# Turning five weights by DMA during the forward chain and loading them plainly later

## The chip, the core and the metric

The kernel runs on one core of one Trainium2 chip. The core has TensorE (PE), VectorE (DVE), ScalarE (ACT), GpSimd (POOL) and SyncE (SP). SP does no arithmetic here; its in-order queue issues DMAs. POOL does copies and issues DMAs as well, from one in-order queue for both. The metric is the device time of one execution in microseconds (us); lower is better. The kernel before took 2935.06 us, the median of three runs from 2926.3 to 2940.95.

## The reference

The reference is a layer of a transformer with a recurrent memory, and its gradients. The forward part, cut to what matters:

```python
h  = x  + A(layernorm(x))          # attention with memory, 64 segments of 32 tokens
h2 = h  + (silu(hn @ w_gate) * (hn @ w_up)) @ w_down     # hn = layernorm(h)
# A, for each segment s:
hs = concat([mem, xs])             # 8 memory tokens + 32 tokens, 448 features
q, k, v = hs @ Wq, hs @ Wk, hs @ Wv                      # 16 heads of 256
o = softmax(mask(q k^T / 16)) v @ Wo
mem = o[:8]                        # goes into segment s + 1
outs.append(o[8:])
```

The kernel returns h2 and the gradients of x, mem0, Wq, Wk, Wv, Wo, w_gate, w_up and w_down for a given `grad_out`. There are 2048 tokens, so 64 segments; Wq, Wk and Wv are 448 x 4096, Wo is 4096 x 448, w_gate and w_up are 448 x 1792, w_down is 1792 x 448; all are bfloat16.

The gradients need weights turned: the gradient of the gate's and the up product's input is `dgp @ w_gate^T + du @ w_up^T`, and that of a segment's input is `dv @ Wv^T + dk @ Wk^T + dq @ Wq^T`. These five turned weights are what the change is about.

## The kernel before

The kernel has four parts, one after another: the forward chain of 64 attention steps, the feed-forward part over 16 tiles of 128 tokens (its forward and its gradients together), the backward chain of 64 steps, and a tail that computes the gradients of the weights. The order of the instructions is written out by hand (`tc.manual_schedule()`); the framework only adds the waits that the data ask for. The parts are Python generators, so that one part's loads and first units stand inside the end of the part ahead of it (`next(feed)`, `next(back)`).

On chip there are four large regions for weights, W[0] to W[3] (`wall` in the profile), and an arena (`arena`) whose layout is a text of names and sizes per part: FWD, FFN, BWD and TAIL. The same bytes serve another purpose in each part, so a later part's write waits for the last reader of an earlier one. In FWD, V_sb lies at 54016 to 58112; in FFN those bytes belong to du and dgp.

**A forward step** (line 785 on, s from 0 to 63; t is the tile of 128 tokens, r the step within it) runs so:

- At its head POOL copies the memory tokens' k and q into kT and qT (L807, L808), and the four memory rows of v are moved by DMA into V_sb (`v_b_rows`, L751), from SP, in step 0 from POOL.
- PE projects k and q (L558), turns them (L572), projects v (L566) and computes the scores (L603). v comes out as 4 x 32 partitions and must stand as 2 x 32 partitions in V_sb, so it is shifted in pieces (`v_shift`): half 0 by POOL (L524) and by DMA from SP (`D_`, L755), half 1 by DMA, ACT and DVE.
- SP stores Kev and Qev to KtokA and QtokA (L858, L859).
- The softmax runs on DVE and ACT (L851 to L867); P is turned on PE (L876) and stored from POOL (L891); SP stores V_sb to Vtok (L894, two DMAs), which the backward chain reads.
- PE multiplies P with V_sb (L910) and the result with Wo (L687), and the sums of the memory tokens go into the next step's input (L616).
- Between these stand units of the next tile's memory-token projections, which fill PE's waits.
- After every fourth step POOL stores OTA and OTB (L959, L960).

**The first border.** `ff.load_turned` (L1010, L1011) stands in step 61 and loads w_down turned; it issues four transposing DMAs from SP. In step 62 the first tile of the feed-forward part is loaded. In step 63 POOL issues the plain loads of w_gate and w_up (`load_first`, L1000, L1002) and SP those of `load_rest`: w_down plainly (L1019), w_gate and w_up turned into W[2] (L1020, L1021). Behind them on SP stands the last step's Vtok store.

**The feed-forward part** takes some 19 us a tile: gate and up (L1105), the down product (L1157), the gradients dgp and du (`grads`, L1168 to L1174), their turning (L1143) and the gradient of the input (`dh_mm`, L1185), then the layer norm's gradient (L215 to L228) and its stores (DH, L1192). From the fourth tile on SP turns OTA blocks by DMA (L1220), and POOL stores them (L1221).

**The second border.** Wo (L1030), Wv, Wk and Wq (`load_back`, L1034) are loaded turned, from the inputs in DRAM, by transposing DMAs on SP's queue, in halves, each as soon as the region under it is free: Wv over gate's and up's weights, Wk over the FFW buffers and w_down, Wq over the turned gate and up. The backward step's `w_pass` (L1392) reads all three. In the backward chain, SP turns V by DMA as well (L1511, two DMAs a step).

The code that the change touches:

Of the kernel before, what the change touches and what calls it, by code (L numbers as in the profile page):

```python
# [10 lines left out]
BF16 = mybir.dt.bfloat16  # L11
# [4 lines left out]
P = 128  # L16
# [84 lines left out]
xtmp:1024x2 x2load:1024x2 P_sb1:1024 S_sb:640x2 maskr:640 maskf:160 hB#1:256"""  # L101
# [164 lines left out]
def run_all(k: _K):  # L266
    nc, tc, ctx = k.nc, k.tc, k.ctx
# [5 lines left out]
    Wq2 = aps["A_Wq"].rearrange("d h e -> d (h e)")  # L273
# [22 lines left out]
    def ps3(n=3):  # L296
# [51 lines left out]
              OTA=OTA, OTB=OTB, OTok=OTok, DHb=DHb, dxnT=dxnTd, memT=memTd, dmemT=dmemTd, memtok=memtok, dmemtok=dmemtok, dQA=dQA, dKA=dKA, dVA=dVA, dQB=dQB, dKB=dKB, dVB=dVB, doutT=doutTd, P_all=P_all)  # L348
    k.dr = dr
# [45 lines left out]
    with tc.manual_schedule():  # L395
# [86 lines left out]
        feed = ffn_phase(k, WT, ff, ffn, mv2, rstd2, {"o": Wo2, "v": Wv2, "k": Wk2, "q": Wq2}, back)  # L482
        k.feed = feed
        forward_chain(k, hA, NWIN, Wq_sb, Wk_sb, Wv_sb, Wo_sb, maskr, fwd, fwd, ff, feed)
# [9 lines left out]
def forward_chain(k: _K, hA, NWIN, Wq_sb, Wk_sb, Wv_sb, Wo_sb, maskr, work, stage, ff, feed):  # L494
# [259 lines left out]
    def D_(out, in_):  # L754
        nc.sync.dma_start(out=out, in_=in_)  # L755

# [28 lines left out]
    for s in range(NSEG):  # L785
# [22 lines left out]
        nc.gpsimd.tensor_copy(out=qT[:, :, SEG:L], in_=T.qB[:, :, r * M:(r + 1) * M])  # L808
        final = s == NSEG - 1
        if not final:  # L810
            v_b_rows(s, V_sb)
# [28 lines left out]
        v_shift(V_sb, Vev, 0, (2, 3), A if final else D_)  # L840
# [16 lines left out]
        v_shift(V_sb, Vev, 1, (0,), G_ if final else D_)  # L857
# [35 lines left out]
        for gg in range(2):  # L893
            nc.sync.dma_start(out=dr["Vtok"][s, gg], in_=V_sb[QB * gg:QB * gg + 48, :])  # L894
# [68 lines left out]

    uo["e3"]()
# [12 lines left out]
class _FFN:  # L977
# [35 lines left out]
    def load_rest(self):  # L1013
# [6 lines left out]
        nc.sync.dma_start_transpose(out=self.WgT, in_=k.aps["B_w_gate"])  # L1020
        nc.sync.dma_start_transpose(out=self.WuT, in_=k.aps["B_w_up"])  # L1021


def load_back(k, v, src, head, c0=0, c1=None):
# [8 lines left out]
    else:  # L1033
        nc.sync.dma_start_transpose(out=v[:, c0:c1, :], in_=src[:, c0 * P:c1 * P])  # L1034


def ffn_phase(k: _K, WT, ff, work, mv2, rstd2, srcs, back):
# [218 lines left out]
    for i in range(NT - 2):  # L1256
# [26 lines left out]
        if i == NT - 3:  # L1283
# [3 lines left out]
            load_back(k, WT["v"], srcs["v"], False, 0, HC)  # L1287
            up(n2)
            load_back(k, WT["v"], srcs["v"], False, HC, 2 * HC)
# [20 lines left out]
    load_back(k, WT["k"], srcs["k"], False, 0, HC)  # L1310
# [3 lines left out]
    load_back(k, WT["k"], srcs["k"], False, HC, 2 * HC)  # L1314
# [8 lines left out]
    load_back(k, WT["q"], srcs["q"], False, 0, 14)  # L1323
    dh_mm(q, (1,))
    load_back(k, WT["q"], srcs["q"], False, 14, 2 * HC)
# [756 lines left out]
```

## Time and profile before

| what | value |
|---|---|
| median of three runs | 2935.06 us |
| profiled execution | 2936.97 us, span 2935.2 us |
| PE busy | 2722.7 us, 93% of the span |
| DVE, ACT, POOL busy | 53%, 37%, 26% of the span |
| granted TensorE clock, mean | 0.980 |
| DMA | 515.86 MB in 652001 packets |
| forward step, steady | about 13.9 us |
| backward step, steady | about 14.5 us |

A profile is one execution. PE counts as busy while a matmul is in flight. A row of the instructions in order of time gives the start and the length in us, the engine and the line, the operation, the tiles written and read, and in brackets the engine's idle time ahead of it with what ended it; SPq stands for SP's queue, and its times are those of issuing, not of the transfer. A row of waits gives the total in us, how many there were, and the longest. A row of stretches gives the busy time and the count of instructions of each engine, then the granted clock, the mean busy share of the 16 DMA engines, and GB/s. The kernel's steps follow one another by data (each memory comes out of the step ahead), so a late piece in a step shows as idle time of PE in that step.

### The profile page before, as it was taken

Reading aid. Unit: us, or ns where it says so; the run is one execution under the profiler, and the core shown is the slowest. Engines: PE = TensorE matmul, PEld = TensorE weight load, DVE = VectorE, ACT = ScalarE, POOL = GpSimd, SP = SyncE. Lnnn points to the kernel's source line nnn. Section 1 sums busy time; section 2 is a strip of 40 time slices with the busy share of each in tenths; the row PEclk is TensorE's granted clock in tenths of the full one; section 3 lists DMA queues with packets and bytes.
Section 4 is the critical chain, followed back from the end, with each engine's and each line's share of the span. In section 5 each row is a group of like instructions: output and inputs, shape, how many; then the busy total and the mean of one; then the engine's idle time right before and its main releaser. Section 6 shows DMA issues by size and latency. Waiting matters only on the chain.

```text
span 2935.2 us, 104407 instructions
## 1 busy us (share of the span) xinstructions
PE 2722.7 (93%) x44384; PEld 1514.8 (52%) x44420; DVE 1561.3 (53%) x4196; ACT 1082.5 (37%) x2880; POOL 762.1 (26%) x1420
## 2 busy tenths in 40 slices
PE   3999999999998799987999999999999999999999
PEld 1555555555554455543555555555555454545454
DVE  4666666666665578874666666666665112222221
ACT  2444444444443455552444444434433111111110
POOL 2222222222222223321222222222222222233222
PEclk7999999999999899998999999999999999999999
DMA  9334434343435899997655655565556999999992
GB/s 273 116 123 134 126 123 137 116 130 122 135 116 140 217 218 233 245 226 166 151 156 153 189 152 161 155 175 152 161 151 215 334 228 227 209 225 241 204 224 69
DMA packets 652001, 515.86 MB, mean 176 GB/s; under 512 B 508592, under 2 KB 558112, under 8 KB 642000
## 3 DMA queue, kind: packets, MB, share of 16 engines
q1 hardware_dynamic: 600640, 309.09, 47.5%
q0 software_dynamic: 50896, 200.09, 20.5%
q8 instruction: 350, 5.73, 0.8%
q14 instruction: 115, 0.94, 0.1%
HBM read 145.89 MB, written 230.33 MB: 128 GB/s over the span
## 4 chain that ended last, share of the span: by engine, by line
PE 69%; DVE 15%; DMA 7%; issue 5%; SPq 2%; ACT 2%; POOL 1%; DVEq 0%; ACTq 0%; POOLq 0%
PE psf L1919 13%; PE psf L558 9%; PE psf L1392 9%; DVE arena L1355 5%; PE psf L687 4%; PE psf L1880 4%; PE psf L1105 3%; PE psf L1701 3%; PE psf L566 3%; PE psf L1364 2%; PE psh L572 2%; PE psf L1932 2%; PE psf L910 2%; PE psf L1399 2%; DMA wall<-in_A_Wv_dram 2%
## 5 line engine op out<-in xcount | busy, mean ns | idle before, releaser
L1919 PE MATMUL psf<-wall,arena 128*128 128x512 bf16 (+1 forms) x1788 | 390.6, 373 | 1.9
L521 ACT CAST arena<-psf 128x512 bf16<-128x512 f32 (+2 forms) x560 | 235.8, 453 | 362.4 <-PE psf L558 251.3
L1392 PE MATMUL psf<-wall,arena 128*32 128x448 bf16 x6144 | 336.8, 361 | 17.0 <-DMA wall<-in_A_Wq_dram 11.9
L1358 ACT CAST arena<-psf 128x256 bf16<-128x256 f32 (+1 forms) x597 | 233.0, 417 | 304.2 <-PE psf L1364 214.0
L558 PE MATMUL psf<-wall,arena 112*32 112x512 bf16 x5120 | 308.9, 384 | 31.0 <-DMA wall<-in_A_Wk_dram 14.0
L1919 PEld LDWEIGHTS <-arena 128*128 128x128 bf16 x1824 | 176.2, 98 | 198.3 <-issue 4.7
L1807 DVE CAST arena<-psf 128x448 bf16<-128x448 f32 (+1 forms) x83 | 54.7, 659 | 418.7 <-PE psf L1919 267.1
L518 DVE CAST arena<-psf 128x512 bf16<-128x512 f32 (+2 forms) x432 | 191.8, 469 | 123.7 <-PE psf L558 83.8
L1392 PEld LDWEIGHTS <-arena 128*32 128x32 bf16 x6144 | 154.9, 98 | 135.7 <-issue 30.7
L558 PEld LDWEIGHTS <-arena 112*32 112x32 bf16 x5120 | 126.4, 97 | 161.8 <-issue 28.2
L1355 DVE CAST arena<-psf 128x256 bf16<-128x256 f32 (+1 forms) x339 | 164.8, 486 | 83.0 <-PE psf L1701 41.8
L1805 ACT CAST arena<-psf 128x512 bf16<-128x512 f32 (+1 forms) x75 | 42.2, 563 | 427.9 <-PE psf L1919 267.0
L566 PE MATMUL psf<-wall,arena 112*32 112x512 bf16 x2560 | 169.2, 385 | 9.4 <-DMA wall<-in_A_Wv_dram 9.4
L1364 PE MATMUL psf<-wall,arena 128*32 128x512 bf16 x2560 | 156.6, 381 | 1.2 <-DVE arena L1404 1.2
L521 ACT COPY arena<-psh 40x160 bf16<-40x160 bf16 (+2 forms) x320 | 119.2, 400 | 94.6 <-PE psh L670 52.8
L1752 POOL COPY arena<-arena 128x32 bf16<-128x32 bf16 x63 | 13.2, 210 | 541.5 <-DVE arena L1404 541.5
L1701 PE MATMUL psf<-arena 40*128 40x40 bf16 x6144 | 146.9, 178 | 3.2 <-issue 1.8
L687 PE MATMUL psf<-wall,arena 128*32 128x224 bf16 x5120 | 147.6, 265 | 1.1 <-issue 1.1
L524 POOL COPY arena<-arena 32x512 bf16<-32x512 bf16 x129 | 77.8, 603 | 267.9 <-ACT arena L521 264.2
L1701 PEld LDWEIGHTS <-arena 40*128 40x128 bf16 x6144 | 125.8, 93 | 33.8 <-issue 16.2
L1355 DVE COPY arena<-arena 32x512 bf16<-32x512 bf16 x384 | 133.8, 349 | 8.8
L1355 DVE COPY arena<-psf 128x192 f32<-128x192 f32 x64 | 22.9, 358 | 215.2 <-ACT arena L1358 215.2
(223 smaller groups left out, 4475.5 us busy)
## 6 DMA issues: line engine op xcount, KB each, us to landing
Vtok<-arena SPq DMA_DIRECT2D x128, 192.0 KB
KtokA<-arena SPq DMA_DIRECT2D x64, 256.0 KB
QtokA<-arena SPq DMA_DIRECT2D x64, 256.0 KB
OTA<-arena POOLq DMA_DIRECT2D x16, 1024.0 KB, 5.2
arena<-QtokA SPq DMA_DIRECT2D x128, 128.0 KB
arena<-KtokA SPq DMA_DIRECT2D x128, 128.0 KB
dVA<-arena POOLq DMA_DIRECT2D x16, 1024.0 KB, 5.2
dKA<-arena POOLq DMA_DIRECT2D x16, 1024.0 KB, 7.2
```

The costliest lines, as they stand in the source:

```text
L518: nc.vector.tensor_copy(out=out, in_=in_)
L521: nc.scalar.copy(out=out, in_=in_)
L558: nc.tensor.matmul(ps[32 * g:32 * g + 32, :], lhsT=stat(kc), rhs=W_sb[0:DB, kc, c0:c0 + HB], start=(kc == 0), stop=(kc == KC - 1))
L566: nc.tensor.matmul(ps[32 * g:32 * g + 32, :].rearrange("t (y d) -> t y d", y=2), lhsT=stat(kc), rhs=wv[:, x, :, half, e, :], start=(kc == ...
L687: nc.tensor.matmul(ps[32 * g:32 * g + 32, 0:2 * DB], lhsT=x, rhs=Wo_sb[:, c, a * 2 * DB:(a + 1) * 2 * DB], start=first, stop=last)
L1355: nc.vector.tensor_copy(out=out, in_=in_)
L1358: nc.scalar.copy(out=out, in_=in_)
L1364: nc.tensor.matmul(ps[32 * g:32 * g + 32, :], lhsT=stat(kc), rhs=WoT_sb[:, kc, c0:c0 + HB], start=(kc == 0), stop=(kc == KC - 1))
L1392: nc.tensor.matmul(pO[32 * g:32 * g + 32, 0:D], lhsT=ch(c), rhs=WT[:, c, :], start=(first and i < 4), stop=(last and i >= MC - 4), skip_gr ...
L1701: nc.tensor.matmul(po[:, n * L:(n + 1) * L], lhsT=lhs[b:b + L, lc:lc + P], rhs=rhs[b:b + L, hh, 0:L], start=True, stop=True)
L1880: nc.tensor.matmul(ps[:, 0:D], lhsT=stat[:, i, c * P:(c + 1) * P], rhs=Y[:, i, 0:D], start=(i == 0), stop=(i == kts - 1))
L1919: nc.tensor.matmul(ps[:, 0:N], lhsT=Hx[:, i, dc * P:(dc + 1) * P], rhs=X[:, i, b * N:(b + 1) * N], start=(i == 0), stop=(i == kts - 1))
```

## The change

In 62 of the first 63 forward steps (all but step 61), behind the step's Vtok store, SP now issues one transposing DMA (`w_turn`): 256 columns of w_gate, w_up, Wv, Wk or Wq (448 x 256, 224 KB) land turned in a new buffer `wturn`, of which there is one. At the head of the next step, behind the two copies L807 and L808, POOL stores that buffer to a new DRAM tensor (`w_store`). There are 7 + 7 + 16 + 16 + 16 = 62 pieces.

At the borders the turned loads of these five weights (`load_rest`, `load_back`) become plain loads from those DRAM tensors, at the same places in the queue of SP. The turned loads of w_down and Wo stay.

In the last two steps, moves leave SP's queue: the v rows of the memory tokens for steps 62 and 63 go out from POOL; in step 62 two pieces of v's half 0 are copied by ACT and one piece of half 1 by POOL, as step 63 did already; and step 63's two Vtok stores go out from POOL, behind P_all.

```diff
+@76032 wturn:1792"""
+    WTd = {w: dram.tile([n, D], BF16, name="WTd_" + w) for w, n in (("g", F), ("u", F), ("v", HD), ("k", HD), ("q", HD))}
+    dr["WT"] = {w: x.rearrange("(c p) d -> p c d", p=P) for w, x in WTd.items()}
...
-            eng = nc.gpsimd if s == 0 else nc.sync
+            eng = nc.gpsimd if s == 0 or s >= NSEG - 2 else nc.sync
             eng.dma_start(out=V_sb[QB * gg + SEG:QB * gg + L, g2 * GF:(g2 + 1) * GF],
...
+    ahead = [(w, c) for w, n in (("g", k.FC), ("u", k.FC), ("v", MC), ("k", MC), ("q", MC)) for c in range(0, n, 2)]
+    held = []
+
+    def w_store():
+        for w, c, b in held:
+            nc.gpsimd.dma_start(out=dr["WT"][w][:, c:c + 2, :], in_=b)
+        held.clear()
+
+    def w_turn():
+        w, c = ahead.pop(0)
+        b = work.tile([P, 2, D], BF16, name="wturn", bufs=1)
+        nc.sync.dma_start_transpose(out=b, in_=wsrc[w][:, c * P:(c + 2) * P])
+        held.append((w, c, b))
...
         nc.gpsimd.tensor_copy(out=qT[:, :, SEG:L], in_=T.qB[:, :, r * M:(r + 1) * M])
+        w_store()
         final = s == NSEG - 1
+        ending = s >= NSEG - 2
...
-        v_shift(V_sb, Vev, 0, (2, 3), A if final else D_)
+        v_shift(V_sb, Vev, 0, (2, 3), A if ending else D_)
...
-        v_shift(V_sb, Vev, 1, (0,), G_ if final else D_)
+        v_shift(V_sb, Vev, 1, (0,), G_ if ending else D_)
...
         for gg in range(2):
-            nc.sync.dma_start(out=dr["Vtok"][s, gg], in_=V_sb[QB * gg:QB * gg + 48, :])
+            (nc.gpsimd if final else nc.sync).dma_start(out=dr["Vtok"][s, gg], in_=V_sb[QB * gg:QB * gg + 48, :])
+        if s != NSEG - 3 and ahead:
+            w_turn()
...
-        nc.sync.dma_start_transpose(out=self.WgT, in_=k.aps["B_w_gate"])
-        nc.sync.dma_start_transpose(out=self.WuT, in_=k.aps["B_w_up"])
+        nc.sync.dma_start(out=self.WgT, in_=k.dr["WT"]["g"])
+        nc.sync.dma_start(out=self.WuT, in_=k.dr["WT"]["u"])
...
-        nc.sync.dma_start_transpose(out=v[:, c0:c1, :], in_=src[:, c0 * P:c1 * P])
+        nc.sync.dma_start(out=v[:, c0:c1, :], in_=src[:, c0:c1, :])
...
-            load_back(k, WT["v"], srcs["v"], False, 0, HC)
+            load_back(k, WT["v"], dr["WT"]["v"], False, 0, HC)
...
```

The other five calls of `load_back` for v, k and q change in the same way.

More of the change, by code (lines that the diff above doesn't have):

```diff
@@ L491, in run_all, with forward_chain @@
     wts.close()
-def forward_chain(k: _K, hA, NWIN, Wq_sb, Wk_sb, Wv_sb, Wo_sb, maskr, work, stage, ff, feed):
+def forward_chain(k: _K, hA, NWIN, Wq_sb, Wk_sb, Wv_sb, Wo_sb, maskr, work, stage, ff, feed, srcs):
     nc, tc = k.nc, k.tc
@@ L962, in forward_chain @@
         late = cur
+    assert not ahead and not held
     uo["e3"]()
```

17 lines of the change are left out of this document (9 added, 8 removed).

## The prediction

> **What bounds the kernel now.** I read the busy time by stretches first, then the waits of TensorE (PE), then the instructions in order of time where PE stood still.
>
> ```profile
> 0.00:50.00 50.00, 11.61 (x92) 4.89 (x93) 22.26 (x70) 7.95 (x17) 9.31 (x23) 0.83 0.98 282
> 120.00:880.00 760.00, 733.67 (x15269) 424.82 (x15261) 496.67 (x1565) 366.88 (x924) 183.35 (x393) 1.00 0.41 126
> 1060.00:1240.00 180.00, 177.03 (x1207) 92.80 (x1206) 146.41 (x245) 99.14 (x178) 59.45 (x112) 0.99 0.95 240
> 1300.00:1350.00 50.00, 29.45 (x448) 15.04 (x446) 19.69 (x49) 12.64 (x34) 6.47 (x13) 0.69 1.09 193
> ```
>
> The columns are the stretch and its length, the busy time of PE, PE's weight loads, DVE, ACT and POOL, the granted clock, the DMA share and GB/s. In the steady forward stretch (120 to 880 us) PE is busy 733.67 of 760 us with the DMA engines at 0.41; in the feed-forward stretch 177.03 of 180. Both are PE-bound, so only their borders can give time back. The second border, 1300 to 1350, has PE busy 29.45 of 50 us at a clock of 0.69 with the DMA engines full. PE's standstills have three places.
>
> First border, the queues of POOL and SyncE (SP), DVE's wait and PE in order of time:
>
> ```profile
> 953.40 0.79 POOL L1000 DMA_DIRECT2D wall<-in_B_w_gate_dram  x1 [0.99 <-PE psf L558]
> ...
> 961.37 22.80 SPq L1020 DMA_TRANSPOSE wall<-in_B_w_gate_dram  x1
> 984.26 12.54 SPq L1021 DMA_TRANSPOSE wall<-in_B_w_up_dram  x1
> 996.90 0.98 SPq L894 DMA_DIRECT2D Vtok<-arena  x2
> ...
> DVE arena L1170 <- DMA Vtok<-arena: 13.7, 1, 13.7
> ...
> 1003.37 3.41 PE L1105 MATMUL psf<-wall 64*128 64x448 bf16 x8 [13.12 <-DVE arena L1118]
> 1006.58 3.11 PE L1143 MATMUL psh<-ident,arena 128*128 128x128 bf16 x28
> ...
> 1021.79 5.88 PE L1105 MATMUL psf<-wall 128*128 128x448 bf16 x32
> 1027.51 1.73 PE L1143 MATMUL psh<-ident,arena 128*128 128x128 bf16 x28
> ```
>
> The turned loads of gate and up hold SP from 961.37 to 996.80. Behind them stands the last step's Vtok store. Its source lies where the feed-forward part writes dgp (L1170), so DVE waits 13.7 us, stops evicting, and PE stands 13.12 us.
>
> The last two forward steps, SP and PE:
>
> ```profile
> 926.85 7.79 SPq L1010 DMA_TRANSPOSE arena<-in_B_w_down_dram  x3
> 936.71 3.76 SPq L751 DMA_DIRECT2D arena<-arena  x4
> ...
> 909.56 0.54 PE L910 MATMUL psf<-arena 104*128 104x80 bf16 x8 [1.01 <-DMA arena<-arena]
> 911.17 3.02 PE L687 MATMUL psf<-wall,arena 128*32 128x224 bf16 x64
> 926.28 1.72 PE L687 MATMUL psf<-wall,arena 128*32 128x224 bf16 x64
> 944.74 0.43 PE L910 MATMUL psf<-arena 104*128 104x80 bf16 x4 [6.00 <-DMA arena<-arena]
> 946.71 3.18 PE L687 MATMUL psf<-wall,arena 128*32 128x224 bf16 x64
> 963.34 3.51 PE L687 MATMUL psf<-wall,arena 128*32 128x224 bf16 x101
> ```
>
> In step 62 the moves into V_sb (L751, then L755) stand on SP behind the turned w_down (L1010), and L910 waits 6.00 us for them. From one L687 block to the next is 15.11 us for step 61, 20.43 for step 62, 16.63 for step 63.
>
> The border to the backward chain, SP, DVE and PE:
>
> ```profile
> 1264.20 28.18 SPq L1034 DMA_TRANSPOSE wall<-in_A_Wv_dram  x2
> 1310.66 11.43 SPq L1034 DMA_TRANSPOSE wall<-in_A_Wk_dram  x1
> 1322.20 15.61 SPq L1034 DMA_TRANSPOSE wall<-in_A_Wq_dram  x2
> ...
> 1309.08 0.69 DVE L228 SCALAR_TENSOR_TENSOR arena<-arena,rstd 128x448 f32<-128x448 f32 x1 [4.19 <-DMA DH<-arena]
> ...
> 1299.36 2.81 PE L1185 MATMUL s_ps<-wall 128*128 128x448 bf16 x14
> 1310.85 1.03 PE L1370 MATMUL psh<-ident,arena 128*128 128x128 bf16 x8 [3.90 <-DVE arena L1355]
> 1332.08 0.94 PE L1392 MATMUL psf<-wall,arena 128*32 128x448 bf16 x8 [4.97 <-DMA wall<-in_A_Wq_dram]
> 1339.97 2.43 PE L1392 MATMUL psf<-wall,arena 128*32 128x448 bf16 x24 [6.96 <-DMA wall<-in_A_Wq_dram]
> 1370.83 3.21 PE L1392 MATMUL psf<-wall,arena 128*32 128x448 bf16 x64
> ```
>
> But for a few loads between, SP is occupied with the turned Wv, Wk and Wq from 1264.20 until 1337.81. PE waits for Wq 4.97 + 6.96 us, and before that 3.90 us for DVE, itself 4.19 us late for a store of DH in the full DMA engines.
>
> **The change part by part.** The sum is made against the profiled execution: 2936.97 us, span 2935.2, so 1.8 us lie around the span. The median shown, 2935.06, is 1.91 lower.
>
> *First border.* Gate and up become two plain loads, and the last Vtok store goes to POOL's queue behind P_all. The standstill of 13.12 us goes. The half clock behind it goes too: eight matmuls of L1105 took 3.41 us where 32 take 5.88 (8: 1.47), and 28 transposes 3.11 where they take 1.73; that is 1.94 + 1.38 = 3.3. Together 16.4 us. What is late next: the plain gate and up, first used by the gradient matmuls behind those 28 transposes, that is at 1006.58 + 3.11 − 16.4 = 993.3. With Wd, Wg and Wu some 8 MB have to come from 953.40 on; at the 282 GB/s of the first 50 us, also a stretch of weight loads, that is 28 us, until 982. It fits by 11 us. Lower bound: nothing of the 3.3, and a few us of wait for these loads; 10.
>
> *End of the forward chain.* For steps 62 and 63 the V moves leave SP: the four row moves (L751) go to POOL's queue, two pieces to ACT, one to POOL. The 6.00 us wait goes. Step 61, less its half-clock loss of 3.02 − 1.72 = 1.30, is 13.8 us; two more ACT copies stand ahead of the exponentials of step 62, and I put 1.2 us for them (POOL's pair of such copies takes 1.26, in the rows of L524 below). So step 62 becomes 15.0 instead of 20.43: 5.4 us. Step 63 may also lose its half clock (101 matmuls in 3.51 us; at 1.72 for 64 it would be 2.7): I take 0.6. Together 6.0, bounds 2 (DMA engines still full of w_down, so that POOL's moves land late) and 7.
>
> *Second border.* Six turned loads become six plain ones, each issued in well under 1 us, so each starts when its target is free. PE's waits of 4.97 and 6.96 go, and DVE's 4.19, which carries the 3.90. The remaining 56 of the L1392 matmuls ran at half clock: 24 in 2.43 us where 64 take 3.21, that is 1.2 us too many in 24 and 2.8 in 56. The first backward step is thin, so I count half, 1.4. Together 4.97 + 6.96 + 4.19 + 1.4 = 17.5, bounds 12 and 20. What is late next: Wq, 3.67 MB, the targets of whose halves become free where the last but one and the last 14 matmuls of L1185 end (1299.4 and 1302.2). At 282 GB/s it needs 13 us and lands at about 1315. Its first use stands at 1332.08 − 4.97 = 1327.1 now, 1323 with DVE's 4.19 gone, perhaps 1320 at full clock: covered by 5 us.
>
> *The price in the forward chain.* 62 of the 63 other steps turn a piece of 224 KB on SP and store it from POOL. One instruction and, one step on, one store each:
>
> ```profile
> 503.44 0.86 SPq L894 DMA_DIRECT2D Vtok<-arena  x2
> 517.79 0.85 SPq L894 DMA_DIRECT2D Vtok<-arena  x2
> 521.54 2.71 SPq L751 DMA_DIRECT2D arena<-arena  x4
> ...
> 509.58 0.40 POOL L808 COPY arena<-arena 128x256 bf16<-128x256 bf16 x1
> 513.41 1.26 POOL L524 COPY arena<-arena 32x512 bf16<-32x512 bf16 x2 [3.44 <-ACT arena L521]
> 521.82 0.40 POOL L808 COPY arena<-arena 128x256 bf16<-128x256 bf16 x1
> 527.70 1.26 POOL L524 COPY arena<-arena 32x512 bf16<-32x512 bf16 x2 [5.48 <-ACT arena L521]
> ...
> 1093.83 5.61 SPq L1220 DMA_TRANSPOSE wall<-OTA  x3
> 1099.88 0.54 POOL L1221 DMA_DIRECT2D OTok<-wall  x1 [7.55 <-DMA wall<-OTA]
> ...
> PE psf L910 <- DMA arena<-arena: 6.2, 11, 1.6
> ```
>
> SP: up's 14 columns took 12.54 us, so a piece of two is 1.8. It goes out behind Vtok, at 518.64, and SP is free at 520.4, before L751 at 521.54: nothing. POOL: the store stands behind L808, from 522.2 on, and waits until the piece has landed; behind it stand POOL's V copies (L524). A turned OTA block of 256 KB, issued at 1093.83 with the DMA engines full, let POOL go at 1099.88, 6.05 us later. So the piece lands by 524.7, the store is issued by 525.2, and L524 starts at 527.70: 2.5 us to spare. In the step that opens a tile the 1 MB OTA store flies beside the piece; 504.30 + 6.05 = 510.4 against 513.41. If the cover were gone, every us would fall on L910. DMA: the moves of L755, issued just before L910 wants them, have no slack. Between 120 and 880 us, 55 steps, L910 waited 11 times for them, 6.2 us in all, in steps of every kind. The piece and its store add transfers to every step, but they lie between Vtok and L524, a few us ahead of L755. I let them double that wait: 62 × 6.2 / 55 = 7.0 us. Bounds: 0 (a gain is excluded, since these steps lose no instruction), and the mean of those waits, 0.56 us, in each step: 35 us.
>
> *The buffer.* The next piece waits for the last store to have left, some 8 us earlier: nothing. If that cover were gone it would hold SP, with L751 behind it.
>
> Sum: −16.4 − 6.0 − 17.5 + 7.0 = −32.9. From 2936.97 that is 2904.1, from the median 2902.2. I say 2902.
>
> **The rivals.** *The V moves come late in every step (slower).* The piece lies in SP's ring ahead of the V row moves, and its store runs beside L755, whose landing ends PE's wait at L910. If each of the 62 steps lost the 1.01 us of the row at 909.56, the price would be 63 us and the time 2937 − 39.9 + 63 = 2960; it decides from 39.9 / 62 = 0.64 us a step on. For it: that wait has no slack. Against: the DMA share of 0.41, with gaps around L755. Chance 0.13.
> The Trainium skill, "DMA: Bandwidth & Descriptors", section "Queues, rings and completion order", bears on this mechanism: each DMA engine takes a queue's descriptors in ring order and alternates between queues packet by packet. No row here shows packets singly.
> On its size the Trainium skill, "TensorE: Matmul & The Clock Gate", section "Why this matters for your kernels", has the rule that only idle gaps above about 3 us bring the half clock back. By it the price stays 63 us; the row behind the 1.01 us gap disagrees, 64 matmuls in 3.02 instead of 1.72 us, and with 1.30 more a step it would be 62 × 2.31 = 143 us and 3040.
>
> *The same mechanism at half strength (no change).* Every step pays the 0.56 us that is the upper bound of the price: 35 us, so 2935 − 39.9 + 35 = 2930. Chance 0.11.
>
> *The plain loads are no faster.* The last two turned halves of Wq, 3.67 MB, went out in 15.61 us, 235 GB/s, hardly below 282; it may be the DMA engines, not the turning, that are slow. At half of 282 Wq lands at 1328 and 8 us of the second border's gain stay away: 2909; with the first border at its lower bound too, 2916. For it: a DMA share above 1 at both borders. Against: SP's order, not bytes, held Vtok and Wq back. Chance 0.11.
>
> **How the numbers follow.** The likeliest case has 0.65: gains within their bounds (24 to 43), a price of 0 to 25 (0.4 us a step). The range is 2888 to 2926: below it all bounds at their best with a little more clock, above it the two first rivals, which hold the part left out. About 0.5% (15 us) is what a measurement can tell from no change. Faster (below 2920) 0.76, same 0.11, slower 0.13.
>
> **What would show it.** Right: no wait of DVE L1170 for Vtok; PE without the 13 us gap; L910 of step 62 not waiting 6 us; no PE wait for Wq; forward steps still 13.9 us on the mean; POOL's wait for the turned piece under 3 us, and L524 not later against ACT. Wrong: L910 waiting for DMA in most steps, a forward stretch longer by 0.6 us a step, or PE waiting for plain weights at either border.

## The result and the profile after

The changed kernel took 2910.26 us, the median of 14 runs from 2896.33 to 2926.14; the kernel before, run beside it, 2934.47 us. The ratio is 0.9926 with a 95% interval from 0.9906 to 0.9946, a gain of 16 to 28 us. A second series of runs gave 2902.97 against 2932.95 us, ratio 0.9898 [0.9871, 0.9924], a gain of 22 to 38 us. The first profiled execution took 2923.15 us with a span of 2921.0, the second has a span of 2898.2.

The stages, in us, read from the rows of TensorE (PE) in order of time. A step is counted from the matmul that puts the mask into its scores; the first border runs from the head of step 63 to the first matmul of the feed-forward input gradient, the second from the first matmul of the backward chain to that of its second step. The table holds all twelve profiles of this study; the kernels of the lower rows are described below.

| profile | steps 1 to 60 | 60 to 63 | first border | feed-forward | second border | backward | tail |
|---|---|---|---|---|---|---|---|
| before | 823.2 | 52.6 | 58.6 | 292.1 | 42.3 | 905.8 | 685.1 |
| before, second | 826.9 | 50.0 | 67.8 | 296.1 | 32.2 | 900.7 | 686.8 |
| after | 830.7 | 45.3 | 48.2 | 291.7 | 23.1 | 905.1 | 700.3 |
| after, second | 827.9 | 45.7 | 49.8 | 291.9 | 23.2 | 899.0 | 686.2 |
| no pieces | 826.0 | 46.0 | 43.9 | 302.1 | 22.9 | 905.4 | 683.9 |
| moves alone | 823.5 | 46.3 | 64.0 | 296.8 | 39.5 | 908.8 | 684.2 |
| last Vtok on SP | 828.7 | 46.5 | 52.4 | 300.9 | 23.2 | 901.0 | 684.3 |
| POOL freed | 826.5 | 46.6 | 43.8 | 293.0 | 22.3 | 898.5 | 683.0 |
| POOL freed, second | 825.5 | 43.9 | 43.4 | 290.3 | 23.6 | 901.8 | 689.8 |
| store late | 825.8 | 44.1 | 49.1 | 293.7 | 22.7 | 902.3 | 684.5 |
| turned twice | 892.3 | 49.5 | 49.8 | 299.7 | 22.5 | 904.9 | 683.5 |
| stored twice | 838.2 | 45.8 | 49.4 | 295.9 | 23.2 | 901.8 | 684.0 |

Averaged over two profiles each, the change gives steps 1 to 60 +4.2, steps 60 to 63 −5.8, the first border −14.2, the second −14.1: together −29.9 us in the stages that it touches. The two spans before and the two after differ by 23.7 us on the mean, less than that, above all because the first profile of the changed kernel has the longest tail of all. Some of this is the variation of one execution: the feed-forward part behind the first border, whose matmuls no edit changes, takes 290.3 to 302.1 us in these profiles.

The same stretches as before, from the first profile of the changed kernel:

```profile
120.00:880.00 760.00, 729.92 (x15128) 422.96 (x15120) 490.40 (x1546) 363.98 (x918) 220.81 (x443) 1.00 0.59 159
1060.00:1240.00 180.00, 180.00 (x1255) 96.11 (x1252) 147.38 (x251) 102.02 (x182) 54.54 (x102) 1.00 0.95 234
1300.00:1350.00 50.00, 42.76 (x891) 23.69 (x887) 28.46 (x76) 18.39 (x64) 7.74 (x17) 0.86 0.66 160
```

In the forward stretch the DMA engines are busy 0.59 of the time instead of 0.41, and PE's busy time has hardly moved. In the last stretch PE is busy 42.76 of 50 us instead of 29.45, at a clock of 0.86 instead of 0.69. That stretch is fixed by the clock, and the border has moved in it, from 1302.1 to 1344.4 us before to 1292.6 to 1315.6. Counted from the start of each border, 50 us hold 42.57 us of busy PE instead of 29.00.

The first border of the changed kernel: GpSimd's (POOL's) queue, SyncE's (SP's) queue, PE.

```profile
955.24 1.03 POOL L754 DMA_DIRECT2D arena<-arena  x2 [7.44 <-PE psf L561]
956.88 1.00 POOL L754 DMA_DIRECT2D arena<-arena  x2 [0.62 <-DMA Vtok<-arena]
...
958.71 0.75 POOL L766 DMA_DIRECT2D WTd_q<-arena  x1
959.45 0.79 POOL L1023 DMA_DIRECT2D wall<-in_B_w_gate_dram  x1
...
947.86 0.53 SPq L1257 DMA_DIRECT2D arena<-arena  x1
...
951.25 0.81 SPq L914 DMA_DIRECT2D Vtok<-arena  x2
...
960.30 1.89 SPq L1042 DMA_DIRECT2D wall<-in_B_w_down_dram  x1
962.29 16.93 SPq L1043 DMA_DIRECT2D wall<-WTd_g  x1
979.31 9.79 SPq L1044 DMA_DIRECT2D wall<-WTd_u  x1
...
979.09 4.61 PE L1128 MATMUL psf<-wall 128*128 128x448 bf16 x16 [1.53 <-DMA wall<-in_B_w_up_dram]
...
989.82 2.81 PE L1180 MATMUL s_ps<-wall 128*128 128x448 bf16 x14 [1.24 <-DMA wall<-in_B_w_down_dram]
992.46 5.88 PE L1128 MATMUL psf<-wall 128*128 128x448 bf16 x32
...
1000.85 1.49 PE L1208 MATMUL s_ps<-wall 128*128 128x448 bf16 x7
```

The 13 us standstill is gone, and L1128 (L1105 before) runs straight through 32 matmuls. In its place are two waits that were not there, for w_up and for w_down, and half-clock blocks around them (16 matmuls of L1128 in 4.61 us, where 32 take 5.88). L1208 is the gradient matmul that reads the turned gate; it has nothing to wait for. In the second profile these waits are 0.6 us for w_up and 3.9 us for w_down. POOL's queue shows why they come: the load of w_gate goes out at 959.45, 6.8 us after the head of step 63 (952.69); before, it was 2.0 us (953.40 and 951.37). Ahead of it stand the V moves (L754), which are new on this queue, and which wait for the Vtok store of step 62 to have read V_sb. That store left SP only at 951.25. Ahead of it on SP stands L1257, a move of a part of the turned w_down: the turned loads had gone out by 943.86, and SP then issued nothing until L1257 at 947.86, which reads what they bring.

The second border of the changed kernel, SP and PE:

```profile
1254.65 4.96 SPq L1057 DMA_DIRECT2D wall<-WTd_v  x2
...
1279.73 0.36 SPq L1057 DMA_DIRECT2D wall<-WTd_k  x1
1291.24 0.39 SPq L1057 DMA_DIRECT2D wall<-WTd_k  x1
1291.73 8.27 SPq L1057 DMA_DIRECT2D wall<-WTd_q  x2
...
1312.62 1.32 PE L1415 MATMUL psf<-wall,arena 128*32 128x448 bf16 x24 [0.48 <-DMA wall<-WTd_q]
```

Of PE's 4.97 + 6.96 us for Wq, 0.48 is left, and none in the second profile. Before, Wq's first half went out at 1322.20, 20.1 us after the first matmul of the backward chain; now it goes out 0.8 us ahead of that matmul (1292.56).

The tail of the first profile is 14 to 17 us longer than in nearly all others. Its waits, and those of the second profile:

```profile
PE psf L1942 <- DMA wall<-dKA: 14.0, 7, 5.6
```

```profile
PE psf L1942 <- DMA wall<-dKA: 2.6, 2, 1.4
```

The tail's instructions are the same in every kernel here; this wait is 14.0 and 2.6 us in the two profiles above, 4.2 in the second with POOL freed and absent in the other nine, of which five also have the new DRAM tensors. I take it as belonging to an execution; what sets it off was not tried.

The second profile of the kernel before shows how far its borders move by themselves:

```profile
960.54 34.97 SPq L1020 DMA_TRANSPOSE wall<-in_B_w_gate_dram  x1
995.60 6.89 SPq L1021 DMA_TRANSPOSE wall<-in_B_w_up_dram  x1
...
1009.08 3.41 PE L1105 MATMUL psf<-wall 64*128 64x448 bf16 x8 [23.18 <-DVE arena L1118]
```

The same turned gate held SP 34.97 us instead of 22.80, and PE stood 23.18 us instead of 13.12. At the second border it was the other way: 32.2 instead of 42.3. The sum of both borders is 100.9 and 99.9 in the two profiles, so the sum is a better measure of the change than either border: 71.2 and 73.0 after. It rests on two profiles of each kernel.

### The profile page after: what moved, and what is told of

Its sections match the earlier page's. It is cut to its first block, busy times and chain, and to the rows that moved or that the text cites. A ratio compares the mean times of both kernels' runs of the same rounds, so it can differ in the third digit from the quotient of the medians.

```text
span 2921.0 us, 104667 instructions
## 1 busy us (share of the span) xinstructions
PE 2724.9 (93%) x44420; PEld 1513.2 (52%) x44420; DVE 1560.8 (53%) x4196; ACT 1083.1 (37%) x2882; POOL 812.9 (28%) x1493
## 3 DMA queue, kind: packets, MB, share of 16 engines
q0 software_dynamic: 56240, 214.84, 22.5%
## 4 chain that ended last, share of the span: by engine, by line
PE 38%; DVE 9%; DMA 4%; issue 3%; ACT 1%; POOL 1%; SPq 1%; ACTq 0%; DVEq 0%; POOLq 0%
PE psf L1942 13%; PE psf L1415 8%; DVE arena L1378 5%; PE psf L1903 3%; PE psf L1724 3%; PE psf L1387 3%; PE psf L1955 2%; PE psf L1422 2%; ACT arena L1381 1%; DVE arena L1710 1%; DVE arena L1707 1%; DVE arena L1704 1%; PE psh L1750 1%; DVE rsum L1706 1%; PE psh L1880 1%
## 5 line engine op out<-in xcount | busy, mean ns | idle before, releaser
L561 PE MATMUL psf<-wall,arena 112*32 112x512 bf16 x5120 | 309.1, 384 | 30.4 <-DMA wall<-in_A_Wk_dram 13.6
L1942 PEld LDWEIGHTS <-arena 128*128 128x128 bf16 x1824 | 176.6, 98 | 214.8 <-issue 22.7
L561 PEld LDWEIGHTS <-arena 112*32 112x32 bf16 x5120 | 126.1, 97 | 161.7 <-issue 27.8
L690 PE MATMUL psf<-wall,arena 128*32 128x224 bf16 x5120 | 150.6, 269 | 0.6 <-issue 0.6
L521 DVE COPY arena<-psh 128x512 bf16<-128x512 bf16 (+2 forms) x336 | 109.5, 342 | 37.0 <-PE psh L575 31.1
L1378 DVE COPY arena<-psf 128x192 f32<-128x192 f32 x64 | 22.9, 357 | 199.1 <-ACT arena L1381 199.1
```

What stands on the lines that cost most here:

```text
L521: nc.vector.tensor_copy(out=out, in_=in_)
L561: nc.tensor.matmul(ps[32 * g:32 * g + 32, :], lhsT=stat(kc), rhs=W_sb[0:DB, kc, c0:c0 + HB], start=(kc == 0), stop=(kc == KC - 1))
L690: nc.tensor.matmul(ps[32 * g:32 * g + 32, 0:2 * DB], lhsT=x, rhs=Wo_sb[:, c, a * 2 * DB:(a + 1) * 2 * DB], start=first, stop=last)
L1378: nc.vector.tensor_copy(out=out, in_=in_)
L1942: nc.tensor.matmul(ps[:, 0:N], lhsT=Hx[:, i, dc * P:(dc + 1) * P], rhs=X[:, i, b * N:(b + 1) * N], start=(i == 0), stop=(i == kts - 1))
```

## The experiments

The theory after the first profile: (a) each border gains because SP's queue is no longer held by turned loads in front of something urgent; (b) the first border gives back some 6 us because POOL's in-order queue in step 63 sends gate and up late; (c) the pieces cost the forward chain 3 to 7 us. Rivals: the moves alone do it; the plain loads alone do it; the lost 6 us are contention between plain loads; the forward price is the late V moves.

### No pieces: what they cost

```diff
-    dr["WT"] = {w: x.rearrange("(c p) d -> p c d", p=P) for w, x in WTd.items()}
+    dr["WT"] = {w: x.rearrange("(c p) d -> p c d", p=P) for w, x in (("g", aps["B_w_down"]), ("u", aps["B_w_down"]), ("v", Wo2), ("k", Wo2), ("q", Wo2))}
...
-        w_store()
...
-        if s != NSEG - 3 and ahead:
-            w_turn()
```

> The changed kernel without its pieces: no forward step turns or stores one, and at the borders the five weights are loaded plainly from other inputs of the same shape and layout (w_down for gate and up, Wo for Wv, Wk and Wq), so the gradients of the inputs are of the wrong weights; the work is the same. Theory 1 (the pieces cost the 7.5 us by which steps 1 to 60 grew): these steps come back to 823 us from 831, the borders stay as in the changed kernel, and the time is about 7 us under it. Theory 2 (the 7.5 us have another cause, as the new layout): they stay at 831. The tail (685 us before, 700 in the changed kernel's profile) has the same instructions in all kernels: if its 15 us belong to the run and not to the change, it will differ from run to run without regard to the kernel.

Measured: 2900.86 us, ratio 0.9906 [0.987, 0.9941]. Steps 1 to 60 take 826.0 us, inside the two values of the kernel before (823.2 and 826.9); the DMA engines are busy 0.40 of the stretch again. The four profiles without pieces average 824.9, the six with one piece a step (after twice, last Vtok on SP, POOL freed twice, store late) 827.5, from 825.4 to 830.7. So the price of 62 pieces is 2.6 us on the mean, and the two groups overlap: a single profile doesn't show it, and neither theory is settled by this one.

The first border is 43.9 us, 4 to 6 less than in the changed kernel, where I had expected no difference. POOL's queue:

```profile
945.03 2.08 POOL L753 DMA_DIRECT2D arena<-arena  x4 [7.41 <-DMA Vtok<-arena]
...
947.93 0.80 POOL L1018 DMA_DIRECT2D wall<-in_B_w_gate_dram  x1
```

The V moves wait for Vtok of step 62 here too. But Vtok leaves SP 2.6 us ahead of the head of step 63 (943.34), there is no piece to store, and gate's load goes out 4.6 us after the head; no wait for w_up or w_down is left.

### The moves alone

The kernel before, with the V moves and the last Vtok store off SP, and the turned loads kept:

```diff
-            eng = nc.gpsimd if s == 0 else nc.sync
+            eng = nc.gpsimd if s == 0 or s >= NSEG - 2 else nc.sync
...
-        v_shift(V_sb, Vev, 0, (2, 3), A if final else D_)
+        v_shift(V_sb, Vev, 0, (2, 3), A if ending else D_)
...
-            nc.sync.dma_start(out=dr["Vtok"][s, gg], in_=V_sb[QB * gg:QB * gg + 48, :])
+            (nc.gpsimd if final else nc.sync).dma_start(out=dr["Vtok"][s, gg], in_=V_sb[QB * gg:QB * gg + 48, :])
```

> The kernel before with the last part of the change alone: the V moves of steps 62 and 63 and the last Vtok store off SyncE's queue; all five weights still loaded turned at the borders. Theory 1 (the stall of the first border was Vtok behind the turned loads): DVE does not wait for Vtok, the 13.1 us standstill of PE goes, but PE then meets the turned gate and up, which land at about 1000 us, a few us late: step 63's head to the first gradient matmul 58.4 us before, about 48 to 50 here, steps 60 to 62 7 us shorter, second border unchanged at 42 us; in all about 15 us under the kernel before. Theory 2 (the turned loads themselves, by their bytes, held the first border): that stretch stays at 55 us or more and only the 7 us are gained.

Measured: 2950.11 us, ratio 1.0035 [0.9988, 1.0082]: no gain. SP and PE at its first border:

```profile
950.32 46.24 SPq L1021 DMA_TRANSPOSE wall<-in_B_w_gate_dram  x1
996.67 11.85 SPq L1022 DMA_TRANSPOSE wall<-in_B_w_up_dram  x1
...
1005.34 5.02 PE L1186 MATMUL s_ps<-wall 128*128 128x448 bf16 x14 [19.19 <-DMA wall<-in_B_w_gate_dram]
```

Steps 60 to 63 take 46.3 us, so that part of the gain comes from the moves. But the Vtok standstill is replaced by one of 19.19 us for the turned gate itself, and the border of 64.0 us is that of Theory 2. In this execution the turned gate held SP for 46.24 us; in the first profile of the kernel before it was 22.80, so whether the 13.12 us for Vtok covered such a wait there too is not shown. The second border stays at 39.5 us, with 11.8 us of waits for Wq: the moves have no part in it. At the first border the moves paid only with plain loads behind them.

### The last Vtok store back on SP

```diff
-            (nc.gpsimd if final else nc.sync).dma_start(out=dr["Vtok"][s, gg], in_=V_sb[QB * gg:QB * gg + 48, :])
+            nc.sync.dma_start(out=dr["Vtok"][s, gg], in_=V_sb[QB * gg:QB * gg + 48, :])
```

> The changed kernel with the last Vtok store back on SyncE's queue, behind the two plain loads. In the changed kernel's trace these two plain loads hold SyncE from 962.3 to 989.1 us although they are plain. Theory 1 (a plain load as large as the queue's room holds the queue nearly as long as a turned one): Vtok goes out at about 989, lands at about 992, and DVE waits for it some 5 to 8 us at dgp, so the first border is 3 to 8 us longer than in the changed kernel. Theory 2 (plain loads free the queue, the move of Vtok is worth nothing beside them): the border is as in the changed kernel, 47.9 us.

Measured: 2906.07 us, ratio 0.9916 [0.9891, 0.9942]. The SP queue and PE of this kernel:

```profile
957.71 14.79 SPq L1043 DMA_DIRECT2D wall<-WTd_g  x1
972.60 5.17 SPq L1044 DMA_DIRECT2D wall<-WTd_u  x1
977.94 7.45 SPq L914 DMA_DIRECT2D Vtok<-arena  x2
...
994.09 3.41 PE L1128 MATMUL psf<-wall 64*128 64x448 bf16 x8 [5.57 <-DVE arena L1141]
```

The old stall returns at 5.57 us and with it the half clock (eight matmuls in 3.41 us). Plain loads hold SP too: 14.79 + 5.17 us here, 16.93 + 9.79 in the changed kernel, against 22.80 + 12.54 for the turned ones. The border of 52.4 us is 3.4 above the changed kernel's mean of 49.0, at the low end of Theory 1. In this profile gate's load went out 3.4 us after the head and PE waited for neither w_up nor w_down, so the delay on POOL moves from one execution to the next as well. So the first border needs both parts: plain loads, and Vtok out from behind them. The runs as a whole don't tell this kernel from the changed one. A kernel with plain loads and all the moves left on SP was not run.

### POOL's queue freed in step 63

```diff
-        w_store()
         final = s == NSEG - 1
+        if not final:
+            w_store()
...
         nc.gpsimd.dma_start(out=dr["P_all"][s], in_=P_sb[0:NR].rearrange("p h n -> p (h n)"))
...
+        if final:
+            w_store()
...
-            (nc.gpsimd if final else nc.sync).dma_start(out=dr["Vtok"][s, gg], in_=V_sb[QB * gg:QB * gg + 48, :])
+            (nc.gpsimd if ending else nc.sync).dma_start(out=dr["Vtok"][s, gg], in_=V_sb[QB * gg:QB * gg + 48, :])
```

> The changed kernel with step 62's Vtok store also issued by GpSimd, and the last piece's store behind step 63's loads of gate and up and its P. Theory 1 (the first border gave 6 us less than predicted because GpSimd's queue in step 63 stands 7.4 us behind step 62's Vtok, and so issues the loads of gate and up 4.7 us later in the step): those loads go out 3 to 5 us earlier in the step, PE's wait of 1.5 us for w_up and its half clock behind it go, and the stretch from step 63's head to the first gradient matmul is 43 to 45 us instead of 47.9. Theory 2 (the DMA engines, shared with the plain loads of the turned weights, deliver no sooner): 47 us or more, the wait stays.

Measured: 2896.56 us, ratio 0.9906 [0.9871, 0.9942]; first border 43.8 us, no wait for w_up or w_down. The plain w_down and the turned gate go out 7.2 and 8.9 us after the head, much as in the changed kernel (7.6 and 9.6); only gate and up are earlier, gate 3.4 instead of 6.8 us after it. So Theory 1 holds: the same loads share the DMA engines, and without the late start of gate and up the waits are gone. It was run again beside the changed kernel:

> The version with POOL's queue freed in step 63 (both Vtok stores of steps 62 and 63 on POOL, the last piece's store behind the loads of gate and up and P_all), now beside the changed kernel on the same chip. Theory 1: it keeps its border of about 44 us against 48, so it is 3 to 5 us faster than the changed kernel, 0.1 to 0.2%, less than the interval of either ratio; ratio to the kernel before 0.990 to 0.992. Rival: the 7 us that its backward chain was shorter by in its first profile are its own too, and it is 10 us faster: ratio 0.988 to 0.989.

> The changed kernel unaltered, a second time, to see which of its stage lengths belong to the change and which to one execution. Theory 1: the tail of 700 us in the first profile (683 to 685 in every other kernel here with the same tail) belongs to that one execution; this profile has a tail of 682 to 687 and a span of about 2907. The border into the feed-forward part is again 47 to 49.5 us, steps 60 to 63 45 to 47, the second border 22 to 24, steps 1 to 60 826 to 831. Rival: the tail is the change's (other addresses of tensors in DRAM, say): about 700 again, and the shorter border is offset by it.

Measured: 2893.46 us, ratio 0.9868 [0.9836, 0.9899], against 2902.97 us and 0.9898 [0.9871, 0.9924] for the changed kernel in the same series. The intervals overlap, so the medians alone don't settle the 9.5 us between them; the borders of 43.4 and 43.8 us against 48.2 and 49.8 do show some 5 us of it. The gain is nearer the rival's 10 us, but not for the rival's reason: the backward chain is 901.8 us here and 899.0 in the changed kernel. POOL's queue of the second run:

```profile
936.00 1.11 POOL L917 DMA_DIRECT2D Vtok<-arena  x2 [0.46 <-ACT arena L524]
939.73 1.04 POOL L754 DMA_DIRECT2D arena<-arena  x2 [2.62 <-PE psf L690]
...
942.85 0.81 POOL L1026 DMA_DIRECT2D wall<-in_B_w_gate_dram  x1
```

Vtok of step 62 leaves at 936.00 and no longer stands behind the turned w_down; the first two V moves follow before step 63 begins (940.49), and gate's load goes out 2.4 us after the head. Of the expectation for the changed kernel's second profile, the borders came as expected, the first with 49.8 us a little above the end given, and the span of 2898.2 is 9 us under it; the tail of 686.2 speaks for the theory that the 700 was one execution's.

### Only the store late

Two edits were made at once in the kernel above. This one has the second alone: the last piece's store behind the loads of gate and up and behind P_all; Vtok of step 62 stays on SP.

```diff
-        w_store()
         final = s == NSEG - 1
+        if not final:
+            w_store()
...
         nc.gpsimd.dma_start(out=dr["P_all"][s], in_=P_sb[0:NR].rearrange("p h n -> p (h n)"))
+        if final:
+            w_store()
```

> The changed kernel with one edit: in step 63 the last piece's store goes out from POOL behind the loads of gate and up and behind P_all, not at the step's head. The Vtok store of step 62 stays on SP behind the turned w_down. Theory 1a: what holds POOL in step 63 is mostly the V moves' wait for that Vtok store (rows at 955.24 to 958.7); then gate's load still goes out 5 to 6 us after the head, PE's wait for up is 0.5 to 1.5 us, and the border is 46.5 to 48. Theory 1b: it is the store of the piece; then gate's load goes out about 3 us after the head, no wait for up, border 44 to 45.

Measured: 2902.25 us, ratio 0.9888 [0.9856, 0.992]; first border 49.1 us. POOL, SP and PE:

```profile
951.44 1.03 POOL L754 DMA_DIRECT2D arena<-arena  x2 [8.84 <-PE psf L561]
...
954.66 0.80 POOL L1026 DMA_DIRECT2D wall<-in_B_w_gate_dram  x1
...
956.25 0.43 SPq L1045 DMA_DIRECT2D wall<-in_B_w_down_dram  x1
956.78 15.41 SPq L1046 DMA_DIRECT2D wall<-WTd_g  x1
...
983.84 4.18 PE L1183 MATMUL s_ps<-wall 128*128 128x448 bf16 x14 [3.15 <-DMA wall<-in_B_w_down_dram]
```

Gate's load is still 7.2 us after the head (947.42), so Theory 1a holds: the V moves, waiting for Vtok of step 62, hold POOL for most of it, though longer than the 5 to 6 us that I gave. Vtok left SP 0.7 us ahead of the head here, against 1.4 and 1.9 in the changed kernel, so this one profile can't price the piece's store of 0.75 us by itself. The border is a us longer than I gave for it, and the wait fell on w_down, not on w_up: gate, up, w_down and the plain turned gate now go out within 3 us of one another and share the engines, and w_down, wanted 24 us after its issue, comes 3 us late. The wait for w_down is the larger of the two in the changed kernel's second profile as well. The row names PE L561 as the releaser of POOL's 8.84 us; where Vtok moved to POOL, in the kernel above, the long wait went away, and the kernel with no pieces has the same wait with Vtok named. In all eight profiles with the V moves on POOL and Vtok of step 62 on SP, the first V move begins 4.0 to 5.2 us after that Vtok's issue. So the named releaser was not the one that mattered. The move of Vtok without the late store was not run.

Over the eight profiles with plain loads and the last Vtok on POOL, the border goes with the time from the head to gate's load. At 2.4, 3.4 and 4.6 us it is 43.4, 43.8 and 43.9 us; from 6.8 to 9.5 us it is 48.2 to 49.8.

### Each piece turned twice

```diff
-        nc.sync.dma_start_transpose(out=b, in_=wsrc[w][:, c * P:(c + 2) * P])
+        for _ in range(2):
+            nc.sync.dma_start_transpose(out=b, in_=wsrc[w][:, c * P:(c + 2) * P])
```

> Every piece is turned twice into the same buffer, one behind the other, so SP's queue holds the second until the first has landed, and the DMA engines carry 62 more pieces of 224 KB in the forward chain. It prices the cover of the steps and the first rival of the prediction. Theory 2a (the forward price is contention in the DMA engines, spread over the step): steps 1 to 60 grow by another 3 to 10 us, to 830 to 840. Theory 2b (there is slack on SP and in the engines; the 4 to 7 us seen are the variation of one execution): 826 to 831, as before. Theory 2c (the V moves have no slack behind the piece, as the rival had it): each us that SP is held falls on L932, 2 to 4 us a step, steps 1 to 60 950 us or more and the time over 3020.

Measured: 2973.0 us, ratio 1.0126 [1.0094, 1.0158]: slower. Steps 1 to 60 take 892.3 us, 63.0 more than the changed kernel's mean of 829.3, or 1.07 us for each of the 59 steps. The expectation missed on both sides: far more than 2a, about half of the least that 2c gave. Waits of PE in this kernel between 120 and 880 us, and then one step on SP, POOL and PE in order of time:

```profile
PE psf L933 <- POOL arena L527: 18.2, 19, 3.8
PE psf L933 <- DMA arena<-arena: 14.8, 26, 1.5
PE psf L933 <- ACT arena L524: 8.8, 11, 1.3
```

```profile
244.53 2.04 SPq L773 DMA_TRANSPOSE arena<-in_B_w_up_dram  x1
246.74 3.17 SPq L754 DMA_DIRECT2D arena<-arena  x4
...
249.95 0.72 POOL L766 DMA_DIRECT2D WTd_u<-arena  x1 [5.45 <-DMA arena<-in_B_w_up_dram]
250.66 1.32 POOL L527 COPY arena<-arena 32x512 bf16<-32x512 bf16 x2
...
252.07 0.30 PE L933 MATMUL psf<-arena 104*128 104x80 bf16 x4 [1.21 <-POOL arena L527]
253.64 0.43 PE L933 MATMUL psf<-arena 104*128 104x80 bf16 x4 [1.26 <-DMA arena<-arena]
...
255.51 3.18 PE L690 MATMUL psf<-wall,arena 128*32 128x224 bf16 x64
```

The second turn waits on SP until the first, issued at 238.46, has landed. The store on POOL comes late, the V copies (L527) behind it become the releaser of PE, the V moves come late as well, and then the clock drops: it is granted at 1.00 until 252 us and at 0.50 from 254 to 258.7, and 64 matmuls of L690 take 3.18 us. In 15 of the 59 steps that block took 2.3 us or more instead of 1.72; in the changed kernel in 2 and none.

### Each piece stored twice

Was it the order or the traffic?

```diff
+    WTe = {w: dram.tile([n, D], BF16, name="WTe_" + w) for w, n in (("g", F), ("u", F), ("v", HD), ("k", HD), ("q", HD))}
+    dr["W2"] = {w: x.rearrange("(c p) d -> p c d", p=P) for w, x in WTe.items()}
...
             nc.gpsimd.dma_start(out=dr["WT"][w][:, c:c + 2, :], in_=b)
+            nc.gpsimd.dma_start(out=dr["W2"][w][:, c:c + 2, :], in_=b)
```

> Each piece is turned once and stored twice from POOL, the second time into a tensor that nothing reads: 62 more stores of 224 KB, no new wait. It is for the 64 us (1.08 us a step) that the doubled turning cost in steps 1 to 60. Theory 3a (those came from order: SP held until the first copy landed, and POOL's store, with the V copies behind it, late by as much): the second store costs POOL 0.8 us a step, which its slack covers, and steps 1 to 60 stay at 827 to 835. Theory 3b (they came from traffic in the DMA engines): 0.5 us a step or more here too, 855 to 890.

Measured: 2915.92 us, ratio 0.9942 [0.9914, 0.9969]; steps 1 to 60 take 838.2 us, 8.9 more than the changed kernel's mean, 0.15 us a step. That is above the 835 of Theory 3a and well below the 855 of 3b. The doubled turning costs seven times as much as a doubled store. The second turning also brings more time of the DMA engines, by the shares in the last section some 1.6 us a step against 0.7, so the two kernels don't part order and traffic cleanly. But that is between two and three times the traffic for seven times the price, and the rows of the doubled turning, where PE waits for POOL's V copies behind the late store, speak for order too.

### The kernel before, again

> The kernel before, unaltered, a second profile, to see how far the stage lengths of one execution repeat. Expected: steps 1 to 60 822 to 826 us, steps 60 to 63 51 to 54, first border 57 to 61, second border 41 to 44, tail 683 to 687. If steps 1 to 60 come to 827 or more, the forward price of the change cannot be told from the variation of one execution.

Measured: 2933.07 us. Steps 1 to 60 took 826.9 us, at the edge that I had set, so one pair of profiles can't show the forward price; the means above can only say that it is a few us. Both borders lie far outside what I expected, 67.8 instead of 57 to 61 and 32.2 instead of 41 to 44. The first is the longer hold of SP by the turned gate, shown in the section on the result. At the second the turned halves of Wv held SP for 16.4 us instead of 28.18, and Wq went out 7.9 us into the backward chain instead of 20.1.

## Why the prediction was right, and where it was not

The time of 2902 us against 2910.26 and 2902.97 measured, and the sum of −32.9 us against −29.9 in the stages concerned, are close. Part of that is terms that offset one another: by the means the two borders gave 5.6 us less than forecast, and the forward price was 2.8 us less. By its own steps:

- **First border, −16.4.** The DVE wait for Vtok and the 13.12 us went, as said. Measured from one profile to the other the border gave 10.4 us, by the means 14.2. Two things are in this. The 13.12 us were one execution's value; the next one had 23.18. And the step that failed is "what is late next … it fits by 11 us". I asked when all five loads of 8 MB would have landed, for the turned gate, the last to be needed, and that fits indeed. I did not ask when the plain w_up and w_down, needed earlier, have to be there. In the changed kernel w_up is wanted at 979.09 − 1.53 = 977.6 and w_down at 988.6, the turned gate only at 1000.85; the two came late because of a move that I had costed only on the queue that it left: the V moves on POOL's queue wait for Vtok of step 62, with the loads of gate and up behind them. A wait of PE for plain weights at a border was one of the prediction's own signs of being wrong, and it came. With that undone the border is 43.6 us on the mean of two runs; the prediction's is 58.6 − 16.4 = 42.2. So what the change removes was right, what comes late next was not, and the lost 5 us have a cause.
- **End of the forward chain, −6.0.** 5.8 by the means, 7.3 from the first profile to the first. The moves alone give 5.0 against the mean of the two profiles before (51.3 to 46.3). PE's wait of 6.00 us in step 62 is gone. Right.
- **Second border, −17.5.** From profile to profile 19.2; by the means 14.1, since the second profile of before had a border of 32.2, with 7.1 us of waits for Wq instead of 11.9 and without the DVE wait for DH and its 3.90 us. The length that the prediction gives, 42.3 − 17.5 = 24.8, was 23.1 and 23.2. The cover of Wq was mis-sized. All of it was forecast to land at about 1315 and its first use to come at 1320, that is 12.9 and 17.9 us after the first matmul of the backward chain (1302.10). In the first profile of the changed kernel the second half landed 20.1 us after that matmul (1312.62 against 1292.56), 7 us later than forecast, and PE had waited 0.48 us for it. Instead of 5 us to spare there were none, and that the wait stayed so short was luck.
- **Forward price, +7.0.** 7.5 from the first pair of profiles, 4.2 by two of each, 2.6 by all profiles with and without pieces. The size lies within the bounds; the way to it was wrong. L910's DMA wait did not double:

```profile
PE psf L932 <- DMA arena<-arena: 7.3, 16, 1.1
```

  This is the second profile of the changed kernel between 120 and 880 us, in which L932 is the former L910: 7.3 us in 16 waits, and 6.5 in 11 in the first, against 6.2 in 11 before. What is left of the price is spread over waits and half-clock steps too small to name one.
- **The cover on POOL and SP.** POOL waits for a piece in about half the steps, at most 3.3 us, where I had said under 3; the V copies still wait for ACT in nearly every step:

```profile
POOL arena L527 <- ACT arena L524: 137.7, 54, 3.8
POOL WTd_k L766 <- DMA arena<-in_A_Wk_dram: 14.3, 9, 3.3
```

  In these rows of the same profile the slack of L527 is 137.7 / 54 = 2.55 us a step. I had worked out 2.5.
- **The rivals.** *V moves late in every step*: not in the changed kernel, but a lateness of this kind is near. Turned twice, it costs 1.07 us a step, above the 0.64 at which it was to decide, and the kernel is 1.26% slower than before; there PE waits more for POOL's V copies (18.2 us) than for V moves (14.8 us). *Half strength*: no. *Plain loads no faster*: in part. At the first border they hold SP 26.7 us against 35.3. Over the second border itself the DMA engines are full before and after (shares of 1.11 and 1.06) and move 190 and 285 GB/s, so there they are faster. But Wq alone took 20.9 us from its issue at 1291.73 to its landing, where the prediction counted 13 and this rival 26; the second half of Wk went out 0.5 us ahead of it. The gain came with the earlier start, 0.8 and 1.3 us ahead of the backward chain instead of 20.1 and 7.9 us into it.
- **The clock.** In the kernel that turns twice 64 matmuls took 3.18 us behind waits of 1.21 and 1.26 us, at a granted clock of 0.50. The Trainium skill, "TensorE: Matmul & The Clock Gate", section "Why this matters for your kernels", asks for no idle gap of TensorE above about 3 us between bursts of matmuls. Read as the only way to the half clock, as the prediction read it, that does not fit these rows: PE was busy 1.49 of the 4 us from 250 to 254, with no gap near 3 us.

A version that beats both kernels by its medians is the one with POOL freed: 2893.46 us, and no wait of PE above 1 us for weights at either border.

## What to carry to other kernels

When an instruction changes queues, cost it on the queue that it joins: read what it will wait for there, and what stands behind it. When several loads are set against one deadline, check the earliest needed of them, not the sum. A long wait that a change removes may have been cover for the next one: price the next one from what it still needs. Take the length of a stall in full DMA engines from more than one execution.

## What the runs showed of the hardware that I had not expected

- A plain load of 1.6 MB with rows of 896 bytes held the queue that issued it for 8.97 to 18.52 us at the first border, over the nine profiles with such a load there, at DMA shares of 0.84 to 1.02. I had counted well under 1 us for such loads at the second border. There, in the first profile of the changed kernel, the halves of Wv took 0.39 and 2.11 us, those of Wk 0.36 and 0.39, and those of Wq 3.41 and 4.76.
- One and the same turned load of w_gate took 22.80, 34.97 and 46.24 us on SP in three profiles. In the two of the kernel before, PE's stall behind it was 13.12 and 23.18 us.
- A turned piece keeps the DMA engines busy two to three times as long as its store. The forward stretch of the second profile of the changed kernel, of the kernel that turns twice and of the one that stores twice:

```profile
120.00:880.00 760.00, 730.65 (x15171) 422.63 (x15170) 493.42 (x1555) 364.98 (x920) 221.32 (x445) 1.00 0.60 159
120.00:880.00 760.00, 700.56 (x13990) 405.12 (x13986) 458.42 (x1430) 338.14 (x850) 206.05 (x412) 0.96 0.66 162
120.00:880.00 760.00, 723.98 (x14976) 418.81 (x14972) 487.57 (x1539) 362.00 (x914) 257.00 (x492) 1.00 0.64 172
```

  This is an estimate from one profile of each. The share times the length of steps 1 to 60, divided by 59, is the time that the engines are busy in a step: 0.41 gives 5.7 us before, 0.60 gives 8.4, 0.66 gives 10.0, and 0.64 gives 9.1. So the second store is 0.7 us, the second turning 1.6, and what is left of the 2.7 us of a piece when its store is taken off is 2.0.
